# Holding the loads of later weight chunks until the first half of the first gate chunk has landed

## The chip, the cores and the metric

One core of a Trainium2 chip. The metric is device time in microseconds (us) of one execution; several executions are taken and the median is quoted. The profile of an execution gives its span, which was 1.8 us shorter than its time here (176.1 against 177.82 us). Ratios are the mean time of one kernel's fast runs over that of the other's fast runs of the same rounds, so they are not quite the ratios of the medians that are quoted beside them. Runs of one call were made on one chip and share the runs of the kernel before.

Terms: TensorE (PE in the profile) does the matrix multiplications (matmuls) and writes them to PSUM, a memory of its own; VectorE (DVE), ScalarE (ACT) and GpSimd (POOL) do the other arithmetic; SyncE (SP) and ScalarE issue the loads. A load is issued by one of these and moved in packets by the DMA engines; it has landed when its semaphore tells that all of it is there. A hold is a wait that is put ahead of an issue.

## The reference

The input x (2048 rows of 512) is normalised; the result is x, plus a diagonal state-space layer, plus a gated feed-forward layer, all in bf16:

```python
def _B_ref(x, w_gate, w_up, w_down):
    return (_gelu(x @ w_gate) * (x @ w_up)) @ w_down       # 512 -> 1376 -> 512

xn = _layernorm(x, axis=-1)
return x + _A_ref(xn, ...) + _B_ref(xn, w_gate, w_up, w_down)
# _A_ref: h[t] = Lam_bar * h[t-1] + (B_bar @ xn[t]);  y = 2 Re(C h) + Dskip * xn
```

What matters here is the start: the first matmuls of the feed-forward layer need rows of x and columns of w_gate and w_up, and all of these come from HBM.

## The kernel before

A small scheduler lists operations with their reads and writes, orders each engine's instructions and adds the semaphore waits. TensorE and SyncE keep program order. SyncE issues nearly all loads, ScalarE two early ones. The weights are cut into chunks of columns: chunk 0 is columns 0 to 384, chunk 1 to 640, chunk 2 to 896, chunk 3 the rest.

```python
ld_x0(0)                                                        # 128 KB each
S.order_behind(ld_x0(1, "scalar", [wrm]), GATE["table"])        # issued by ScalarE
ld_wg0(0, "sync")                                               # gate chunk 0, first half, 192 KB
S.order_behind(ld_wg0(1, "scalar", [wrm]), GATE["table"])       # second half, by ScalarE
ld_x0(2)
ld_w(WU, WUc, ins["B_w_up"], 0)                                 # up chunk 0, 384 KB
ld_x0(3)
for ci in (1, 2):
    ld_w(WG, WGc, ins["B_w_gate"], ci)                          # 256 KB each
    ld_w(WU, WUc, ins["B_w_up"], ci)
# ... cut; then on SyncE: chunk 3 of both (480 KB each), the transpose of the
# parameters (tr_par), the transposes of the first input block, the next input block
```

The start of TensorE's program, in its order (shortened):

```python
PE(fwarm, ...)                              # 7 matmuls on constants, 512 columns   (L902)
fill(5)                                     # 5 more, 128 columns                   (L909)
cent_T(0, tb, "AA"); cent_T(1, [wb])        # 8 transposes of input tiles 0 and 1   (L662)
GT_mm(0, r, ...)                            # 8 matmuls on gate chunk 0             (L687)
fill(4)                                     #                                       (L909)
GT_mm(1, r, ub[1, r], [0])                  # 8 matmuls on gate chunk 0             (L687)
GT_mm(0, 0, ub[0, 0], [1])                  # 4 matmuls: the FIRST ON UP CHUNK 0    (L687)
cent_T(2, tb)                               # 4 transposes of input tile 2          (L662)
# ... cut: further units on chunk 0, then chunks 1 and 2; later L812, L786 (other
# feed-forward matmuls), L723 (state-space input), L853 (down projection)
```

Of the kernel before, what the change touches and what calls it, by code (L numbers as in the profile page):

```python
# [361 lines left out]
def build(nc, ins, out):  # L362
    with ExitStack() as es:
# [11 lines left out]
        WG = A.alloc("WG", [KD, F], BF16)  # L375
# [5 lines left out]
        WGc = [Buf("WGc%d" % i, "sbx", 10 * i, 10 * i + 1) for i in range(4)]  # L381
# [99 lines left out]
        def ld_w(W, Wc, src, ci, queue="sync", after=()):  # L481
            f0, f1 = FCH[ci]
            return S.dma(lambda e: e.dma_start(W.ap[:, :, f0:f1], src[:, f0:f1].rearrange("(k p) f -> p k f", p=128)),
                         512 * (f1 - f0) * 2, writes=[Wc[ci]], tag="ld_w", queue=queue, after=after)

        def ld_x0(j, queue="sync", after=()):
            return S.dma(lambda e, j=j: e.dma_start(X[j].ap, x2[128 * j:128 * (j + 1), :]), 128 * 1024, writes=[X[j]], tag="ld_x0", queue=queue, after=after)  # L487
        WG0h = [Buf("WG0h%d" % n, "sbx", n / 2, (n + 1) / 2) for n in range(2)]

        def ld_wg0(n, queue, after=()):  # L490
            return S.dma(lambda e: e.dma_start(WG.ap[:, 2 * n:2 * n + 2, 0:384],  # L491
                                        ins["B_w_gate"][256 * n:256 * (n + 1), 0:384].rearrange("(k p) f -> p k f", p=128)),
                  192 * 1024, writes=[WG0h[n]], tag="ld_w", queue=queue, after=after)
        ld_x0(0)
        S.order_behind(ld_x0(1, "scalar", [wrm]), GATE["table"])
        ld_wg0(0, "sync")
        S.order_behind(ld_wg0(1, "scalar", [wrm]), GATE["table"])
        ld_x0(2)
        ld_w(WU, WUc, ins["B_w_up"], 0)
        ld_x0(3)  # L500
        for ci in (1, 2):
            ld_w(WG, WGc, ins["B_w_gate"], ci)
            ld_w(WU, WUc, ins["B_w_up"], ci)

        def load_par():
# [506 lines left out]
def bass_parallel_sum__ssm_conv_s5__geglu_ffn__prompt_kernel(  # L1012
    nc: bass.Bass,
    A_x: bass.AP,
    A_Lambda_re: bass.AP,
    A_Lambda_im: bass.AP,
    A_B_re: bass.AP,
    A_B_im: bass.AP,
    A_C_re: bass.AP,
    A_C_im: bass.AP,  # L1020
    A_log_dt: bass.AP,
    A_Dskip: bass.AP,
    B_x: bass.AP,
    B_w_gate: bass.AP,
    B_w_up: bass.AP,
    B_w_down: bass.AP,
    out: bass.AP,
):
    ins = {
        "A_x": A_x, "A_Lambda_re": A_Lambda_re, "A_Lambda_im": A_Lambda_im,  # L1030
        "A_B_re": A_B_re, "A_B_im": A_B_im, "A_C_re": A_C_re, "A_C_im": A_C_im,
        "A_log_dt": A_log_dt, "A_Dskip": A_Dskip,
        "B_w_gate": B_w_gate, "B_w_up": B_w_up, "B_w_down": B_w_down,
    }
    build(nc, ins, out)
# [28 lines left out]
```

## Time and profile before

| | before |
|---|---|
| median of the first three runs | 177.92 us (177.74 to 178.09) |
| span of the profiled run | 176.1 us |
| TensorE busy | 172.0 us, 98% |
| wait for up chunk 0 ahead of its first matmul | 0.30 us |
| landing of up chunk 0 (issued at 2.17 us) | 7.09 us |

From the page of the kernel before: part 1 (busy us, share of the span, instructions) and part 4 (the chain that ended last, by engine).

```profile
PE 172.0 (98%) x876; PEld 84.1 (48%) x891; DVE 162.2 (92%) x283; ACT 90.2 (51%) x169; POOL 10.3 (6%) x25
PE 94%; DMA 3%; SPq 1%; issue 1%; DVE 0%
```

The chain is matmuls nearly throughout. Its one DMA piece is at the start. From the chain of the kernel before over its first 45 us; columns are start, duration, what:

```profile
2.17 4.92 DMA arena<-in_B_w_up_dram
7.09 0.05 issue
7.13 0.50 PE PS L687 x4
...
10.40 8.21 PE PS L687 x40
```

So the first use of up chunk 0 at 7.13 us sets when the rest starts. The timeline of the kernel before for SyncE (start, duration, what) shows the issues; a duration is the time that SyncE took to hand the load over:

```profile
2.17 0.43 SPq L483 DMA_DIRECT2D arena<-in_B_w_up_dram  x1
2.64 0.51 SPq L487 DMA_DIRECT2D arena<-in_A_x_dram  x1
3.19 0.45 SPq L483 DMA_DIRECT2D arena<-in_B_w_gate_dram  x1
3.68 0.51 SPq L483 DMA_DIRECT2D arena<-in_B_w_up_dram  x1
4.23 0.51 SPq L483 DMA_DIRECT2D arena<-in_B_w_gate_dram  x1
4.78 1.47 SPq L483 DMA_DIRECT2D arena<-in_B_w_up_dram  x1
6.30 1.23 SPq L483 DMA_DIRECT2D arena<-in_B_w_gate_dram  x1
```

The first line is up chunk 0, the second input tile 3, then chunks 1, 2 and the gate part of 3. The issue of the sixth took 1.47 us, where 0.5 is usual. The timeline of the same kernel for TensorE in this stretch (start, duration, operation, count; in brackets idle time before it and what ended it):

```profile
3.62 0.46 PE L909 MATMUL PS<-const-bfloat16-1.0 128*128 128x128 bf16 x5
4.27 0.66 PE L662 MATMUL PS<-arena 128*128 128x128 bf16 x8 [0.19 <-DVE arena L921]
5.12 0.82 PE L687 MATMUL PS<-arena 128*128 128x192 bf16 x8 [0.19 <-ACT arena L669]
5.78 0.40 PE L909 MATMUL PS<-const-bfloat16-1.0 128*128 128x128 bf16 x4
6.01 0.82 PE L687 MATMUL PS<-arena 128*128 128x192 bf16 x8
7.13 0.50 PE L687 MATMUL PS<-arena 128*128 128x192 bf16 x4 [0.30 <-DMA arena<-in_B_w_up_dram]
```

The last line is the wait that the change is about. And three stretches of 1 us of the kernel before (busy time per engine, granted clock, DMA share, GB/s):

```profile
4.00:5.00 1.00, 0.74 (x10) 0.45 (x8) 1.00 (x3) 0.41 (x2) 0.00 (x0) 1.00 0.91 246
5.00:6.00 1.00, 0.88 (x12) 0.91 (x13) 0.93 (x4) 0.74 (x2) 0.60 (x2) 1.00 1.00 292
6.00:7.00 1.00, 0.83 (x11) 0.60 (x8) 0.89 (x5) 0.00 (x0) 0.30 (x1) 1.00 1.06 316
```

The DMA engines are busy all through.

### The profile page before, as it was taken

To read this page: it belongs to the slowest core of one execution; us is meant where nothing else is said; L and a number is where in the kernel's file an instruction comes from. 1 tells how busy PE (TensorE), PEld (TensorE's weight loads), DVE (VectorE), ACT (ScalarE), POOL (GpSimd) and SP (SyncE) were. 2 spreads that over 40 slices of the span, in tenths; PEclk is the share of its full clock that TensorE was granted. 3 is DMA by queue.
4 is the path that set the end of the run, shared out by engine and by line. 5 is a ranking of instruction groups with operands and counts; after the bars stand their busy time and mean duration, and the time that the engine had idled before them with its cause. 6 is when DMAs were issued, how large, how long until landed. Compare 5 with 4: busy or idle time off the path is not lost.

```text
span 176.1 us, 2489 instructions
## 1 busy us (share of the span) xinstructions
PE 172.0 (98%) x876; PEld 84.1 (48%) x891; DVE 162.2 (92%) x283; ACT 90.2 (51%) x169; POOL 10.3 (6%) x25
## 2 busy tenths in 40 slices
PE   7899999999999999999999999999999999999995
PEld 3754464444644444444644444444464444444454
DVE  6978999986999999879999999999999999999981
ACT  5565568899876899002676793000667790000000
POOL 3212040210000000010000000000000000000000
PEclk9999999999999999999999999999999999999999
DMA  5996999984997000012015000002101000000142
GB/s 175 310 305 137 208 227 152 116 156 100 238 308 151 4 0 2 0 46 73 4 37 111 3 0 0 4 0 79 40 0 30 4 0 0 0 0 0 34 147 63
DMA packets 33396, 14.36 MB, mean 82 GB/s; under 512 B 23688, under 2 KB 33384, under 8 KB 33384
## 3 DMA queue, kind: packets, MB, share of 16 engines
q1 hardware_dynamic: 32944, 13.87, 35.0%
q10 hardware_dynamic: 440, 0.33, 0.6%
q8 instruction: 7, 0.11, 0.3%
q14 instruction: 5, 0.04, 0.1%
HBM read 6.46 MB, written 2.10 MB: 49 GB/s over the span
## 4 chain that ended last, share of the span: by engine, by line
PE 94%; DMA 3%; SPq 1%; issue 1%; DVE 0%
PE PS L853 37%; PE PS L812 32%; PE PS L723 16%; PE PS L687 6%; PE PS L786 3%; DMA arena<-in_B_w_up_dram 3%; SPq L487 0%; PE PS L662 0%; SPq L491 0%; DVE arena L871 0%
## 5 line engine op out<-in xcount | busy, mean ns | idle before, releaser
L853 PE MATMUL PS<-arena 128*128 128x512 bf16 (+3 forms) x317 | 65.9, 366 | 0.3
L812 PE MATMUL PS<-arena 128*128 128x512 bf16 x258 | 57.5, 379 | 0.3
L853 PEld LDWEIGHTS PS<-arena 128*128 128x128 bf16 (+1 forms) x323 | 30.8, 98 | 35.2
L812 PEld LDWEIGHTS PS<-arena 128*128 128x128 bf16 x264 | 25.8, 98 | 30.4
L756 DVE TENSOR_TENSOR_SCAN arena<-arena 128x512 bf16<-128x512 f32 x32 | 38.8, 1254 | 0.0
L827 ACT ACTIVATE arena<-PS 128x512 bf16<-128x512 f32 x33 | 19.7, 598 | 37.0 <-PE PS L812 34.5
L723 PE MATMUL PS<-arena 128*128 128x512 bf16 x125 | 27.8, 379 | 0.2
L831 ACT ACTIVATE arena<-PS 128x512 bf16<-128x512 f32 x33 | 19.7, 597 | 4.7 <-PE PS L812 4.3
L845 ACT ACTIVATE PS<-arena 128x512 f32<-128x512 bf16 (+2 forms) x17 | 9.6, 581 | 20.4 <-PE PS L853 19.7
L723 PEld LDWEIGHTS PS<-arena 128*128 128x128 bf16 x128 | 12.5, 98 | 14.9
L727 ACT ACTIVATE arena<-PS 128x512 bf16<-128x512 f32 x32 | 17.6, 595 | 2.3 <-PE PS L723 2.3
L871 DVE TENSOR_TENSOR arena<-PS,arena 128x512 bf16<-128x512 f32 (+2 forms) x17 | 10.9, 654 | 5.0 <-PE PS L853 4.5
L833 DVE TENSOR_TENSOR arena<-arena 128x512 bf16<-128x512 bf16 x33 | 13.0, 417 | 1.6 <-ACT arena L831 1.4
L687 PE MATMUL PS<-arena 128*128 128x192 bf16 (+2 forms) x80 | 13.0, 315 | 0.5 <-DMA arena<-in_B_w_up_dram 0.3
L613 DVE BATCH_NORM_STATS2 arena<-arena 128x6 f32<-128x512 bf16 x16 | 10.3, 682 | 0.9 <-DMA arena<-in_A_x_dram 0.9
L743 DVE TENSOR_TENSOR arena<-arena 128x4096 bf16<-128x4096 bf16 (+1 forms) x5 | 9.2, 1859 | 0.5 <-ACT arena L608 0.5
L687 PEld LDWEIGHTS PS<-arena 128*128 128x128 bf16 x80 | 7.1, 98 | 5.4 <-DMA arena<-in_B_w_up_dram 0.5
L745 DVE TENSOR_TENSOR arena<-arena 128x4096 bf16<-128x4096 bf16 (+1 forms) x5 | 9.2, 1860 | 0.5 <-ACT arena L609 0.5
L696 ACT ACTIVATE arena<-PS,arena 128x192 bf16<-128x192 f32 (+1 forms) x16 | 6.7, 448 | 5.0 <-PE PS L687 4.0
L768 DVE TENSOR_TENSOR arena<-arena 128x4096 bf16<-128x4096 bf16 x4 | 9.2, 2290 | 0.1
L769 DVE TENSOR_TENSOR arena<-arena 128x4096 bf16<-128x4096 bf16 x4 | 9.1, 2286 | 0.0
L699 DVE SCALAR_TENSOR_TENSOR arena<-PS,arena 128x192 bf16<-128x192 f32 (+1 forms) x16 | 6.6, 443 | 0.9 <-ACT arena L696 0.9
(84 smaller groups left out, 109.4 us busy)
## 6 DMA issues: line engine op xcount, KB each, us to landing
out_dram<-arena SPq DMA_DIRECT2D x15, 128.0 KB, 1.7
arena<-in_A_x_dram SPq DMA_DIRECT2D x3, 512.0 KB, 5.1
arena<-in_B_w_down_dram SPq DMA_DIRECT2D x1, 1280.0 KB, 7.9
arena<-in_B_w_gate_dram SPq DMA_DIRECT2D x2, 256.0 KB, 5.4
arena<-in_B_w_up_dram SPq DMA_DIRECT2D x2, 256.0 KB, 5.7
arena<-in_B_w_gate_dram SPq DMA_DIRECT2D x1, 480.0 KB, 5.8
arena<-in_B_w_up_dram SPq DMA_DIRECT2D x1, 480.0 KB, 5.9
arena<-arena SPq DMA_TRANSPOSE x25, 2.6
```

Of the source, the lines that this page charges most:

```text
L613: return (V(lambda e: e.bn_stats(ST[tt].ap, X[tt].ap), d_dve_1x(512), [X[tt]], [ST[tt]], "bnst"), V(lambda e: e.bn_aggr(MVt[b][j].ap, ST[t ...
L687: ins_ = e.matmul(dst, XCd(j, k), WGU[:, us[0]:us[-1] + 1, k, f0:f1], start=(k == 0), stop=(k == KD - 1))
L723: ins_ = e.matmul(PS[bank][:, :], BBT[c][dk].ap[:, 128 * s:128 * (s + 1)], XNT[b].ap[:, dk, :], start=(dk == 0), stop=(dk == KD - 1))
L727: GATE["evBu"] = ACT(lambda e, bank=bank, k3=k3, s=s, c=c: e.activation(SSc[k3][s][c].ap, PS[bank][:, :], ACTF.Copy), d_act(512), [BANK[ba ...
L756: V(lambda e, g=g, rb=rb, init=init: e.tensor_tensor_scan(g.ap, rb, g.ap, init, ALU.mult, ALU.add), d_dve_scan(512), [g, PA[RRr]] + ([CARc ...
L812: ins_ = e.matmul(PS[bank][0:m, c0:c1], W.ap[:, dk, 128 * ft:128 * ft + m], XNT[b].ap[:, dk, c0:c1], start=(dk == 0), stop=(dk == KD - 1))
L827: GATE["last_gelu"] = ACT(lambda e, bg=bg, kk=kk, m=m: e.activation(GG[kk].ap[0:m, :], PS[bg][0:m, :], ACTF.Gelu_apprx_tanh), d_act(512), ...
L831: ACT(lambda e, bu=bu, kk=kk, m=m: e.activation(UPB[kk].ap[0:m, :], PS[bu][0:m, :], ACTF.Copy), d_act(512), [BANK[bu]], [UPB[kk]], "evU")
L833: V(lambda e, kk=kk, m=m, ft=ft, k2=k2: e.tensor_tensor(HTt[k2][ft].ap[0:m, :], GG[kk].ap[0:m, :], UPB[kk].ap[0:m, :], ALU.mult), d_dve_tt ...
L845: ACT(lambda e: e.activation(PS[bank][:, c0:c1], X[tt].ap[:, c0:c1], ACTF.Copy), d_act(c1 - c0), [X[tt]], [BANK[bank]], "seed")
L853: ins_ = e.matmul(PS[bank][:, c0:c1], l_[:, 128 * j:128 * (j + 1)], r_[:, c0:c1], start=False, stop=last and n == len(ops) - 1, skip_group ...
L871: V(lambda e: e.tensor_tensor(OUTB[ko].ap[:, c0:c1], PS[bank][:, c0:c1], XD[tt].ap[:, c0:c1], ALU.add), d_dve_1x(c1 - c0), [BANK[bank], XD ...
```

## The change

The intent: loads that are needed only from 10 us on should not share the DMA engines with those that are needed first. The load of gate chunk 1, and with it everything behind it on SyncE, is issued only once the first half of gate chunk 0 has landed.

```diff
-        ld_wg0(0, "sync")
+        gate0 = ld_wg0(0, "sync")
         S.order_behind(ld_wg0(1, "scalar", [wrm]), GATE["table"])
         ld_x0(2)
         ld_w(WU, WUc, ins["B_w_up"], 0)
         ld_x0(3)
         for ci in (1, 2):
-            ld_w(WG, WGc, ins["B_w_gate"], ci)
+            ld_w(WG, WGc, ins["B_w_gate"], ci, after=[gate0] if ci == 1 else ())
             ld_w(WU, WUc, ins["B_w_up"], ci)
```

The order of instructions on every engine stays as it was; one wait is added on SyncE.

## The prediction

> **What bounds the kernel now.** TensorE. The page's busy table has PE at 172.0 of 176.1 us (98%), and the chain that ended last is 94% PE and 3% DMA. The DMA part is the load of the first up chunk (384 KB): in the chain over the first 45 us it is issued at 2.17 us and followed for 4.92 us, landing at 7.09. The first matmul that needs it waited 0.30 us (waits view); no other matmul of that stretch waited for a load. From 7.13 to about 30 us the timeline shows PE without a gap, so 0.30 us (0.17%) is about all that earlier loads could give.
>
> **What the change does.** Every engine's instruction order stays. One semaphore wait is added on SyncE, ahead of the second gate chunk; everything behind it on SyncE moves with it. The first half of the first gate chunk is issued at 1.20 and lands 2.7 us later, at about 3.9. Before, the second gate chunk was issued at 3.19. So its issue and those of the next three loads come about 0.75 us later (3.95 to 5.5).
>
> **Does the first up chunk land sooner?** The Trainium skill, page "DMA: Bandwidth & Descriptors", section "Queues, rings and completion order", says each DMA engine consumes descriptors in ring order. The trace agrees: adding the GB/s of 1 us windows gives 1.20 MB by 6.0, 1.51 by 7.0, 1.86 by 8.0 us. Everything issued up to the first up chunk (with ScalarE's two loads) is 1.18 MB, moved by 6.0: landed at 7.09. Up to the fourth input tile 1.31 MB, by 6.4: landed at 7.5. Up to the second gate chunk 1.57 MB, by 7.2: landed at 8.3. Each lands 1.1 to 1.2 us after its place in the line, so loads behind it took nothing. Expected gain: 0 to 0.1 us.
>
> **Does the hold cost anything?** By 3.95 us only 0.65 MB of the 1.31 MB issued ahead has moved; it lasts to 6.4. First bytes of the first load appear about 1.2 us after issue, so those of the held chunk are there at about 5.2: no hole in the DMA activity. Also, the issue of the third up chunk took 1.47 us and the next 1.23 (the others 0.5), which I read as a full queue; the delay should be absorbed there, and the last chunks go out at about 6.3 and 7.6 as before. Even a full 0.75 us is safe: the second chunks landed at 8.3 and 9.1 and are needed at 10.24; the third landed at 9.9 and 10.8, needed at about 15; the last landed at 13.5, needed at 18.66.
>
> **Prediction.** 177.9 us, 8 in 10 between 177.5 and 178.3. Chances: faster by over 2% 0.005, within 2% 0.99, slower by over 2% 0.005.
>
> **What would show each step right or wrong.** Right: SyncE is idle from about 3.15 to 3.95 in the timeline; the first up chunk lands at 7.1 and the matmul's wait stays near 0.3 us; DMA share stays near 1 between 3 and 8 us; issue times of the loads meet those of before by about 6.3 to 7.6 us. Wrong: the wait vanishes (later issues did disturb the load), or DMA share dips at 5 to 7 us and a matmul waits at 10.24 for a second chunk.
>
> **What would make it wrong.** If building descriptors for later loads slows those in flight, the up chunk gains up to 0.3 us. If the full queue doesn't absorb the delay, the input transposes go out later and VectorE's chain, 92% busy, could shift.

## The result, and the profile after

| | before | after |
|---|---|---|
| median, 6 runs each | 178.00 us (177.73 to 178.21) | 177.51 us (177.38 to 177.98) |
| ratio of fast runs | | 0.998, interval 0.9963 to 0.9996 |
| span of the profiled run | 176.1 | 176.2 (the slowest of its six runs: spans were 175.7 to 176.2) |
| first later chunk issued | 3.19 us | 3.87 us |
| first packets of that chunk | 5.87 us | 5.82 us |
| up chunk 0 landed | 7.09 us | 7.15 us |
| parameter transpose landed, behind all the weights | 13.66 us | 13.83 us |

The time is the same within 2%. The time of the first packets, like other packet times below, is from the packet records of the trace. They are told apart by size: chunks 1 and 2 are the only loads of the start that move in packets of 512 bytes.

The timeline of the kernel after for SyncE, the same seven loads:

```profile
2.16 0.43 SPq L483 DMA_DIRECT2D arena<-in_B_w_up_dram  x1
2.64 0.51 SPq L487 DMA_DIRECT2D arena<-in_A_x_dram  x1
3.87 0.38 SPq L483 DMA_DIRECT2D arena<-in_B_w_gate_dram  x1
4.29 0.51 SPq L483 DMA_DIRECT2D arena<-in_B_w_up_dram  x1
4.85 0.51 SPq L483 DMA_DIRECT2D arena<-in_B_w_gate_dram  x1
5.39 0.89 SPq L483 DMA_DIRECT2D arena<-in_B_w_up_dram  x1
6.33 1.23 SPq L483 DMA_DIRECT2D arena<-in_B_w_gate_dram  x1
```

The hold delays four issues by 0.6 to 0.7 us, the sixth issue then takes 0.89 instead of 1.47 us, and the seventh starts at 6.33 against 6.30. The delay is gone there. TensorE, after:

```profile
3.71 0.74 PE L909 MATMUL PS<-const-bfloat16-1.0 128*128 128x128 bf16 x5
4.29 1.03 PE L662 MATMUL PS<-arena 128*128 128x128 bf16 x8
5.25 1.23 PE L687 MATMUL PS<-arena 128*128 128x192 bf16 x8
6.32 0.40 PE L909 MATMUL PS<-const-bfloat16-1.0 128*128 128x128 bf16 x4
6.56 1.15 PE L687 MATMUL PS<-arena 128*128 128x192 bf16 x12
```

The wait for the up chunk is not in these lines, although the chunk landed no sooner. (The last line joins the 8 matmuls on gate chunk 0 with the 4 on the up chunk, which start at 7.21.) The reason stands in the first three lines: eight transposes took 1.03 us, not 0.66. In this execution the matmuls ran at about half speed until about 6.1 us, in the profile of before only until about 3.6 us. TensorE itself was late, and the chunk was there when it came. (The granted clock of 1.00 in the views is no evidence against this: time for which a trace has no clock record is counted as full clock, and the records of these two traces start only at the turn, at 3.52 us before and 6.14 us after.) The same three stretches, after:

```profile
4.00:5.00 1.00, 1.00 (x12) 0.89 (x10) 1.00 (x3) 0.27 (x1) 0.00 (x0) 1.00 0.97 281
5.00:6.00 1.00, 1.00 (x9) 0.77 (x7) 0.46 (x3) 0.96 (x3) 0.57 (x2) 1.00 1.02 338
6.00:7.00 1.00, 1.00 (x15) 0.99 (x13) 0.69 (x1) 0.00 (x0) 0.32 (x1) 1.00 1.03 293
```

There is no hole in the DMA activity. And of the page of the kernel after, parts 1 and 4 (the profile of the kernel before lacks 15 matmul records, x876 against x891, so its busy time reads lower):

```profile
PE 173.6 (99%) x891; PEld 84.9 (48%) x891; DVE 162.3 (92%) x283; ACT 90.3 (51%) x169; POOL 9.8 (6%) x25
PE 99%; DVE 0%; issue 0%
```

The DMA piece has left the chain, and the span did not get shorter: the chain's start is now TensorE's own slow matmuls. Reading only "the DMA share of the chain fell from 3% to 0" would have suggested a gain. These two profiles cannot tell what the hold does, so more were taken.

### The profile page after: what moved, and what is told of

Its sections match the earlier page's. It is cut to its first block, busy times and chain, and to the rows that moved or that the text cites. A ratio compares the mean times of both kernels' runs of the same rounds, so it can differ in the third digit from the quotient of the medians.

```text
span 176.2 us, 2504 instructions
## 1 busy us (share of the span) xinstructions
PE 173.6 (99%) x891; PEld 84.9 (48%) x891; DVE 162.3 (92%) x283; ACT 90.3 (51%) x169; POOL 9.8 (6%) x25
## 4 chain that ended last, share of the span: by engine, by line
PE 99%; DVE 0%; issue 0%
PE PS L853 37%; PE PS L812 32%; PE PS L723 16%; PE PS L687 7%; PE PS L786 3%; PE PS L902 2%; PE PS L662 1%; PE PS L909 0%; DVE arena L871 0%
## 5 line engine op out<-in xcount | busy, mean ns | idle before, releaser
L812 PE MATMUL PS<-arena 128*128 128x512 bf16 x264 | 58.1, 379 | 0.0
L812 PEld LDWEIGHTS PS<-arena 128*128 128x128 bf16 x264 | 25.8, 98 | 30.4
L723 PE MATMUL PS<-arena 128*128 128x512 bf16 x128 | 28.1, 379 | 0.0
```

What stands on the lines that cost most here:

```text
L723: ins_ = e.matmul(PS[bank][:, :], BBT[c][dk].ap[:, 128 * s:128 * (s + 1)], XNT[b].ap[:, dk, :], start=(dk == 0), stop=(dk == KD - 1))
L812: ins_ = e.matmul(PS[bank][0:m, c0:c1], W.ap[:, dk, 128 * ft:128 * ft + m], XNT[b].ap[:, dk, c0:c1], start=(dk == 0), stop=(dk == KD - 1))
```

## The experiments

Two theories were put against each other. **Order of issue**: the DMA engines take the loads in the order of issue, so loads behind up chunk 0 take nothing from it, and the hold does nothing. **Sharing** (the rival): later loads do slow it, the hold makes it land sooner, and the 0.2% is a real gain. A further possibility came from the profiles: what differs between executions is when the matmuls turn fast.

### Nulls and repeats

A null is a kernel run against itself. `before_again` and `before_3` are the kernel before, `after_again` and `after_3` the changed one, with no edit.

> The kernel before, unchanged, against itself: it measures what counts as no difference. The theory of the prediction (loads are served in the order of issue, so the hold changes nothing) expects a ratio within 0.998 to 1.002, and that the profiled executions differ from each other, in when the matmuls turn from slow to fast, by as much as after and before differ. The rival (the 0.2% gain is real and comes from the hold) expects this ratio at 1.000 within 0.001 and the changed kernel at 0.998 again in the same call.

> The changed kernel, unchanged, on the chip of the other runs of this call. No-effect theory: ratio 0.999 to 1.001, interval holding 1; the first up chunk lands at 7.1 us as before. Rival of a real gain of 0.2 to 0.4 us: ratio about 0.998 with an interval below 1, and in its profile the first up chunk lands, or the first matmul on it starts, at 6.7 to 6.9 us.

> The kernel before, unchanged, once more: a third profile of the start without a hold, and another measure of no difference. Landings of the first up chunk without a hold were 7.09, 7.10 and (without fillers) 6.84 us. Expected: 6.8 to 7.15 us, ratio 0.9985 to 1.0015.

> The changed kernel, unchanged, once more. Its landings of the first up chunk were 7.15, 6.69 and (without fillers) 6.83 us; its ratios 0.998 and 1.0003. If the hold has no effect on the first up chunk: landing again anywhere in 6.65 to 7.15 us and a ratio of 0.9985 to 1.001. If it gains about 0.2 us: landing below 6.9 us and a ratio of about 0.9985 with its interval below 1. The first packets of the held chunk are expected at 5.8 to 5.9 us in either case, as without a hold.

| run | ratio to before | interval |
|---|---|---|
| before_again | 1.0007 | 0.9994 to 1.0019 |
| before_3 | 0.9994 | 0.9978 to 1.0010 |
| after (first comparison) | 0.998 | 0.9963 to 0.9996 |
| after_again | 1.0003 | 0.9990 to 1.0017 |
| after_3 | 0.9988 | 0.9970 to 1.0005 |

The 0.998 of the first comparison did not come back as a clear difference. The up chunk landed at 6.69 and 6.78 us in the two new profiles of the changed kernel, 7.10 and 6.87 in those of before: the range without a hold (6.87 to 7.10) lies inside that with it (6.69 to 7.15). The 7.1 us that the theory of order of issue expected of `after_again` was missed: 6.69 is where the rival had it, though the ratio was not. First packets of the held chunk came at 5.88 and 5.77 us with the hold, 5.84 and 5.83 without, as expected. The seventh issue stood at 6.02 and 5.96 us with the hold, 6.22 and 6.05 without: it was not delayed in any of them.

### A later chunk moved ahead of up chunk 0 (g1_ahead)

```diff
-        ld_w(WU, WUc, ins["B_w_up"], 0)
+        ld_w(WG, WGc, ins["B_w_gate"], 1); ld_w(WU, WUc, ins["B_w_up"], 0)
...
-            ld_w(WG, WGc, ins["B_w_gate"], ci)
+            if ci == 2: ld_w(WG, WGc, ins["B_w_gate"], ci)
```

> The second gate chunk (256 KB) issued just ahead of the first up chunk, no hold: it moves one load from behind to ahead in the line and changes nothing else. Theory of order of issue: the first up chunk lands later by the time that 0.26 MB takes at 0.31 to 0.35 MB/us, 0.75 to 0.85 us, at about 7.9 us; the first matmul on it waits about 1.1 us and the time rises by 0.7 to 0.9 us (ratio about 1.0045). Rival (loads in flight share the engines, so a load behind costs about as much as one ahead): it lands within 0.2 us of 7.1 us and the ratio stays within 1.001.

Measured: up chunk 0 landed at 7.80 us, 0.71 later than in the profile of before; ratio 1.0040 (1.0026 to 1.0054), median 178.50 us. The waits of TensorE in its first 45 us (engine, line, waited for: us in total, times, longest), then its timeline:

```profile
PE PS L687 <- DMA arena<-in_B_w_up_dram: 0.9, 1, 0.9
```

```profile
7.84 0.50 PE L687 MATMUL PS<-arena 128*128 128x192 bf16 x4 [0.93 <-DMA arena<-in_B_w_up_dram]
```

The first matmul on the chunk started at 7.84 instead of 7.13 us, and the span grew by the same 0.71 us (176.79 against 176.07). A quarter of a megabyte ahead in the line costs about its full transfer time. All the loads behind it together cost about 0.5 us, as the next runs show. Place in the line is the larger effect for one load, and the hold does not change it.

### The hold made longer (hold_up0, hold_g0b)

The wait is put on after the orders have been made, so that every engine's order stays. `hold_up0` waits for up chunk 0 itself, `hold_g0b` for the second half of gate chunk 0.

```diff
-        ld_w(WU, WUc, ins["B_w_up"], 0)
+        up0 = ld_w(WU, WUc, ins["B_w_up"], 0)        # hold_g0b: g0b = the half that ScalarE issues
...
-            ld_w(WG, WGc, ins["B_w_gate"], ci)
+            GATE["g%d" % ci] = ld_w(WG, WGc, ins["B_w_gate"], ci)
...
-        S.schedule()
+        S.schedule(); GATE["g1"].deps.append(up0)    # hold_g0b: g0b
```

> The hold made much longer: the second and later weight chunks are held back until the first UP chunk has landed (about 7.1 us), so that no later load at all can share the DMA engines with it. Every engine keeps its order. Theory of order of issue: the first up chunk still lands at 7.0 to 7.2 us, so nothing is gained, and the DMA engines now stand empty for about 1 us around 7 us; the second chunks land at about 10.2 and 11.0 us, the matmul at 10.24 waits 0.5 to 1 us, and the time rises by 0.5 to 1.2 us (ratio 1.003 to 1.007). Rival (later loads take bandwidth from the first up chunk): it lands at 6.8 us or earlier, the wait of 0.30 us before its first matmul is gone.

> A hold between the two tried: until the second half of the first gate chunk (issued by ScalarE) has landed, at 5.2 to 5.6 us; every engine keeps its order. First packets of the held chunk follow its issue by about 1.05 us (7.58 after 6.54 in the run with the longest hold), so at 6.3 to 6.7 us, when the line ahead of it is done. Theory of order of issue: up chunk at 7.1 us, ratio 1.000 to 1.003 because all later loads, the parameter transpose at the end of the line among them, shift by 0.1 to 0.5 us. Rival: up chunk at 6.5 to 6.6 us as with the longest hold; the wait of TensorE is gone, and the time falls by up to 0.3 us unless the later shift takes it back: ratio 0.998 to 1.002.

| | before | hold_g0b | hold_up0 |
|---|---|---|---|
| gate chunk 1 issued | 3.19 us | 5.20 | 6.54 |
| its first packets | 5.87 | 6.24 | 7.58 |
| up chunk 0 landed | 7.09 | 6.27 | 6.52 |
| parameter transpose landed | 13.66 | 14.63 | 16.13 |
| median | (177.83 in the call of hold_g0b, 177.74 in that of hold_up0) | 178.25 | 179.76 |
| ratio | | 1.0026 (1.0004 to 1.0048) | 1.0118 (1.0101 to 1.0136) |

Here the theory of order of issue falls short: with nothing issued behind it, the up chunk landed at 6.27 and 6.52 us (and 6.68 in `nofill_hold_g0b` below), not at 7.0 to 7.2. The mean of the three, 6.49, is about 0.5 us below that of the kernels without a hold (7.09, 7.10, 6.87 and, below, 6.84: mean 6.98). So loads behind do slow it: all three landings lie below all four, though with one profile of each kernel the size is uncertain. But this gain is useless to the kernel: both are slower. The stretches of hold_up0:

```profile
5.00:6.00 1.00, 1.00 (x9) 0.80 (x8) 0.93 (x4) 1.00 (x3) 0.35 (x2) 1.00 1.06 358
6.00:7.00 1.00, 1.00 (x13) 0.97 (x12) 0.93 (x4) 0.02 (x1) 0.55 (x1) 1.00 0.19 66
7.00:8.00 1.00, 1.00 (x17) 1.00 (x15) 0.96 (x4) 0.07 (x1) 0.00 (x0) 1.00 0.21 28
```

358 GB/s with no load behind, then a hole from about 6.5 to 7.6 us. What the hole cost was not what had been expected: no matmul at 10.24 us waited for a weight chunk. The waits of TensorE in hold_up0:

```profile
PE PS L812 <- ACT arena L696: 0.8, 1, 0.8
PE PS L723 <- DMA arena<-arena: 0.8, 1, 0.8
```

The first comes from the parameter transpose, which is the last of the line. It landed at 16.13 us instead of 13.66. GpSimd computes with the parameters first; in VectorE's program an operation on its result stands in front of the multiplications that free PSUM. The timelines of GpSimd and VectorE in hold_up0 show it:

```profile
16.27 1.01 POOL L555 TENSOR_TENSOR arena<-arena 128x4 bf16<-128x4 f32 x1 [5.74 <-DMA arena<-arena]
17.38 0.16 DVE L556 TENSOR_TENSOR arena<-arena 128x4 f32<-128x4 bf16 x1 [2.73 <-POOL arena L555]
```

VectorE stood idle for 2.73 us, ScalarE behind it for 1.26, and TensorE waited 0.77 us ahead of L812. The second wait is for a transposed block of the input, whose own load went out behind all this. In hold_g0b only that second kind is left:

```profile
PE PS L723 <- DMA arena<-arena: 0.6, 1, 0.6
```

The hole also cost more than its own length: in hold_g0b the packets of chunks 1 and 2 went on until 11.42 us where they ended at 10.21 in before, though their first came only 0.37 us later. Why the DMA engines were slower after the restart is left open.

### Without the four fillers (nofill_before, nofill_hold, nofill_hold_g0b)

```diff
-        fill(4)
+        pass
```

on the kernel before, on the changed kernel, and on `hold_g0b`. It brings TensorE to the up chunk about 0.23 us sooner, so that a landing can show in the time.

> The kernel before without the four filler matmuls that stand ahead of the first matmul on the first up chunk: TensorE is ready for that chunk about 0.2 us sooner, so the wait shows the landing more plainly, whatever the phase in which the matmuls turn fast. If the time up to there is set by the landing at 7.1 us, as in both profiles of the kernel before, the wait grows by about 0.2 us (to 0.3 to 0.5 us) and the time does not move: ratio 0.999 to 1.001. If it is set by TensorE itself, the time falls by about 0.2 us (ratio 0.999).

> The changed kernel without the same four fillers. Theory of order of issue alone: the first up chunk lands at 7.1 us, ratio equal to that of nofill_before within 0.001. Rival (loads behind it do slow it, in the 0.4 us or so in which some DMA engines have already gone on to the next chunk while others still work on this one; one of two profiles of the changed kernel had it land at 6.69): it lands at 6.6 to 6.9 us and the time is 0.2 to 0.4 us below nofill_before (ratio about 0.998).

> The same middle hold without the four fillers: a second look at where the first up chunk lands with nothing issued behind it, with the gain not hidden by the fillers. Theory of order of issue: landing at 7.1 us, ratio as hold_g0b within 0.001. Rival: landing at 6.5 to 6.6 us and TensorE starts on it at 6.6 to 6.8 us, 0.3 to 0.5 us sooner than in the kernel before; ratio 0.997 to 0.9985 if nothing later gives way, and about 1.000 if the shift of later loads takes it back.

| | ratio to before | up chunk 0 landed | first matmul on it | span |
|---|---|---|---|---|
| nofill_before | 1.0004 (0.9988 to 1.0019) | 6.84 us | 6.88 us | 175.83 us |
| nofill_hold | 0.9995 (0.9981 to 1.0009) | 6.83 | 6.88 | 175.82 |
| nofill_hold_g0b | 1.0024 (0.9999 to 1.0050) | 6.68 | 6.85 | 175.78 |

With and without the hold the first two profiles agree to 0.01 us in the landing and in the span. The rival had expected 0.2 to 0.4 us between them; the ratios differ by 0.0009, less than either interval. The profile of nofill_hold_g0b caught its fast end: its six runs spread from 177.51 to 179.21 us, so in most of them the gain is taken back and more, presumably by a late input block as in the profile of hold_g0b; the slower five were not profiled.

### Up chunk 0 one place further ahead (up_first, nofill_up_first)

```diff
-        ld_x0(2)
         ld_w(WU, WUc, ins["B_w_up"], 0)
+        ld_x0(2)
```

without a hold; the second also without the four fillers.

> No hold; the first up chunk is issued ahead of the third input tile (128 KB) instead of behind it, so it stands 0.13 MB further ahead in the line. Theory of order of issue: it lands 0.13 MB / 0.31 MB per us = 0.4 us sooner, at 6.4 to 6.7 us, with all the later loads behind it as before; the third tile lands at 6.0 to 6.4 us instead of 5.2 to 6.2. The wait of 0.30 us of TensorE goes; what remains is when TensorE itself is ready (6.9 to 7.2 us, by when the matmuls turn fast): ratio 0.998 to 1.000, and slower if the third tile's statistics then hold VectorE up.

> The same without the four fillers, so that TensorE is ready 0.2 us sooner: the first up chunk at 6.4 to 6.7 us and the first matmul on it at 6.5 to 7.0 us. Ratio 0.9975 to 0.9995. This is the most that the start can give by this route; if it stays within 0.999 to 1.001 the landing of the first up chunk is not what sets the time any more.

Measured: ratios 1.0047 (1.0031 to 1.0064) and 1.0054 (1.0036 to 1.0071): slower. The up chunk landed at 6.84 and 6.41 us, one of the two as expected. The risk that the expectation had named came true: input tile 2, now behind the up chunk, landed at 7.16 us in up_first where it had come at 5.18 in before, and the statistics of that tile held VectorE up. From the timeline of up_first:

```profile
7.18 0.69 DVE L613 BATCH_NORM_STATS2 arena<-arena 128x6 f32<-128x512 bf16 x1 [1.71 <-DMA arena<-in_A_x_dram]
8.54 0.40 PE L662 MATMUL PS<-arena 128*128 128x128 bf16 x4 [0.55 <-DVE arena L921]
```

The transposes of that tile, next on TensorE after the first matmuls on the up chunk, started at 8.54 instead of 7.48 us, and the span grew by the same 1.06 us (177.13 against 176.07). Of nofill_up_first, one of six runs took 372.69 us, and the profile is of that one: a slow run with the matmuls at about half speed to the end (mean 679 ns at L812, 379 before). It is left out of the ratio; the other five took 178.36 to 179.07 us. The landing of 6.41 us is from this slow run and is not leant on.

### One line through nine of the profiles

Subtracting the start of the first matmul on up chunk 0 from the span gives the rest of the kernel. "Fast from" is when the start-to-start time of the matmuls drops to half.

| profile | fast from | up chunk landed | first matmul on it | span | rest |
|---|---|---|---|---|---|
| before | 3.6 us | 7.09 | 7.13 | 176.07 | 168.94 |
| before_again | 4.2 | 7.10 | 7.15 | 176.18 | 169.03 |
| before_3 | 6.3 | 6.87 | 7.33 | 176.27 | 168.94 |
| after | 6.1 | 7.15 | 7.21 | 176.22 | 169.01 |
| after_again | 5.1 | 6.69 | 6.89 | 175.82 | 168.93 |
| after_3 | 6.5 | 6.78 | 7.42 | 176.35 | 168.93 |
| nofill_before | 3.9 | 6.84 | 6.88 | 175.83 | 168.95 |
| nofill_hold | 5.6 | 6.83 | 6.88 | 175.82 | 168.94 |
| g1_ahead | 3.7 | 7.80 | 7.84 | 176.79 | 168.95 |

Six of these nine traces hold clock records (no view of the profile lists them). The record of full clock starts at 3.52 us in before, 6.36 in before_3, 6.14 in after, 6.61 in after_3, 5.64 in nofill_hold and 3.72 in g1_ahead, within about 0.1 us of the column.

In all nine the rest is 168.93 to 169.03 us. Left out are the runs in which something later gave way too (the rest is 169.64 in hold_g0b, 170.56 in hold_up0, 169.63 in up_first), nofill_hold_g0b (168.93) and the slow run. The first matmul starts 0.04 to 0.06 us after the landing, or when TensorE is done with what stands before it, whichever is later. So a hold can gain only in executions in which the matmuls turn fast early enough, and then about the 0.30 us of the wait seen in before; in before_3, also without a hold, there was no wait left to remove.

## Why the prediction was right

The measured median (177.51 us) lies just inside the range of 177.5 to 178.3, and "within 2%" was right. That it lies inside by 0.01 us is luck; the medians of the two later calls, 177.80 and 177.58 us, lie inside it too. Of the mechanism, point 4 was mis-sized and point 5 was wrong. Point by point:

1. *TensorE bounds the kernel and 0.30 us is about all that an earlier up chunk could give.* Right, and firmer than was known: span = first matmul on the up chunk + 168.9 us in nine profiles, and g1_ahead shows it from the other side (0.71 us later, 0.71 us longer).
2. *The hold moves four issues by about 0.75 us and is absorbed where the queue is full.* Right: 0.61 to 0.68 us, then the seventh issue at 6.33 against 6.30. That the queue is full is a reading of the 1.47 and 0.89 us; no run was made to test it. The long holds fit it: there the same issue took 0.51 us.
3. *No hole in the DMA activity.* Right. The Trainium skill's page "DMA: Bandwidth & Descriptors", section "Latency and other measured facts", gives about 600 ns to the first byte of a load issued by SyncE. In hold_up0 the first packets came 1.04 us after the issue began and 0.66 after it ended (6.54, 6.92 and 7.58 us), so trace and page agree if the time is counted from the end of the issue, which the page does not say. (The prediction's 1.2 us for the first load was too long as well: 1.03 us by the packet records, 0.74 to 1.77.) With a hold that ends at 3.87 us the held chunk could have moved from about 4.9 us (estimate: 3.87 + 1.04), and its turn came only at 5.8.
4. *Loads behind the up chunk take nothing from it.* **This step was mis-sized.** It was argued from bytes counted per microsecond, which can show the order but not how fast the line moves. With nothing issued behind it, the chunk landed about 0.5 us sooner (6.49 against 6.98 us, three and four profiles). For the change itself the conclusion stood: with its short hold the held packets start as early as without (5.77 to 5.88 against 5.83 to 6.04 us), and the mean landing of four profiles with it is 6.86 us (7.15, 6.69, 6.78, 6.83), 0.12 below that without, inside the scatter. The predicted landing of 7.0 to 7.1 us was too narrow: executions differ by 0.45 us.
5. *The wait stays near 0.3 us.* Wrong in the profile, though not because the load came sooner: the wait was hidden by matmuls that turned fast at 6.1 instead of 3.6 us. The Trainium skill's page "TensorE: Matmul & The Clock Gate", Part 1, says that the window that decides this is free-running, so that the moment differs from run to run. The profiles agree that it differs with no edit at all: 3.6, 4.2 and 6.3 us in three profiles of the kernel before. The clock records fit a fixed window too: the stretches of full clock last 170.67 or 174.08 us, which differ by 3.41 us and are 50 and 51 times that. What sets the moment in a given run no run shows.
6. *Even a full 0.75 us delay of the later loads would be safe.* Not tested at that size. The argument looked at when the weight chunks are needed, and hold_g0b shows that this is not the tightest: with the last weight loads shifted by 1 us, no matmul waited for a weight, but the next input block, which goes out behind the small parameter transpose at the end of the same line, came late: TensorE waited 0.6 us for it, and the time rose by 0.26%. The late parameter transpose cost time only with the longest hold.

What stays open: whether the change gains about 0.1 us. The three comparisons gave 0.998, 1.0003 and 0.9988, the two nulls 1.0007 and 0.9994. The plain means are 177.69 us (17 runs with the change) and 177.83 (47 runs of the kernel before, all calls together, three chips or more), 0.14 us apart. A gain of that size fits the slightly earlier mean landing; it is not shown. Also open is how later loads slow the up chunk. Both the packets of the next chunk that run beside its last ones and the issuing itself fell into the same microseconds, and no run separates them. The packet records say that the first can hardly be all: by 5.75 us, before any packet of a later chunk had started, the loads up to input tile 3 had moved 1.10 to 1.13 MB in the four profiles without a hold, 1.09 to 1.19 MB in the four with the short one and 1.17 to 1.24 MB in the three with a long one. But up_first, without a hold, had moved 1.17 MB too.

No version tried beats both kernels.

## What to carry to other kernels

Here, delaying the issue of loads clearly helped the one in front only when the held packets came no sooner than the last packets of that load; the shorter hold changed the issue times and, within the scatter, not the transfers, and the longer ones opened a hole whose cost fell on what stood at the end of the line: a small transpose and the next input block. So look at the end of the line before holding it. To bring a load sooner, count the bytes ahead of it, and look at what the load that you push back was feeding. When a wait vanishes from a profile and the time stays, check whether the waiter came later before crediting the load, and take several profiles before explaining a few tenths of a microsecond.

## What the Trainium skill lacked or had wrong

- "TensorE: Matmul & The Clock Gate", Part 1: it gives about ±500 ns for the moment when matmuls turn fast. With seven identical warm-up matmuls from 0.77 us on, the profiles have it from 3.6 to 6.5 us, a far wider spread. (The same Part itself has the wider spread in a note: one kernel had 6, 11 or 14 slow matmuls in different runs.) The granted clock that the views print is 1.00 on both sides of it, because the traces have clock records from the turn on (8 of 14) or none; matmul spacing shows it.
- "DMA: Bandwidth & Descriptors", "Queues, rings and completion order": it describes the order but not what a full line behind costs a load in flight. Here a load of 384 KB landed about 0.5 us sooner with nothing issued behind it (mean 6.49 against 6.98 us).
- The same page has nothing on the issuing engine being held up: the issue of up chunk 2 took 1.12 to 1.47 us in the seven profiles without a hold and 0.51 in the three with a long hold, and this absorbed a delay of 0.7 us.
- No page has a run that stays slow to its end: one execution of 372.69 us in a kernel that otherwise takes 178.4 to 179.1, with matmuls at a mean of 679 instead of 379 ns. The granted clock printed for it, 1.00, says nothing: its trace has no clock record.
